# Attention and two gated feed-forward layers on one core: decay inputs in one transfer, decay matmuls apart from score matmuls, two operand differences in other buffers, and a new order

## The chip, the cores and the metric

The kernel runs on one core of one Trainium2 chip. The metric is device time in microseconds of one execution. Before the change it took 926.08 us, the median of three runs (925.92, 926.08 and 928.21 us).

## The reference

Inputs are q, k and v for 4 batches, 8 heads, 576 positions and head size 64, and s with one number per position. Each head computes

```python
scores = (q @ k.T) / sqrt(64)
cum    = cumsum(max(s, 0))                    # along the sequence
scores = where(causal, -1e9, scores + minimum(-(cum[i] - cum[j]), 0))
attn   = exp(scores - max) ; attn /= (sum + 1e-9)
out    = attn @ v
```

The result, 2304 tokens of 512 numbers, passes through two feed-forward layers, 512 to 2048 to 512: the first with h * clip(h + 3, 0, 6) / 6, the second with h * tanh(softplus(h)). All is float32. The word "decay" below means the term with cum.

## The kernel before

Nothing in the program is ordered where it is written. Each piece of work (a transfer, a matmul group, one vector operation) is recorded by `add` as a node with an engine, a cost, a priority, the nodes it depends on and the buffers it takes. `Plan.run`, at build time, walks a modelled clock and picks the ready node of the lowest priority number on each engine; where a node may run on ScalarE or VectorE it also picks the engine. The table `T` holds the priorities' offsets: `p0` to `p5` and `s0` to `s5` place the groups of attention heads, `xo1` and `lead1` place the operands and the weight sums of the first large matmul block, `w0` and `w1` the weights, and so on. The order that results is fixed; on the chip each engine runs its own list in order, and semaphores hold an instruction until what it needs is there. All loads and stores are issued from the SP queue, also in a fixed order. Where the model sees TensorE idle in its first 70 us, it puts in matmuls on the identity (L362), up to 24 in a place, whose result is not used.

Weights come as 64-bit floats. `rebuild` loads 512 KB of words into one of two buffers named `wraw` (L465) and makes float32 of it: one operation on ScalarE or VectorE (L434), then L444 and L461 on VectorE. Every operand of a large matmul is then split into a high part (a copy to fp32r, L367 on ScalarE or L371 on VectorE) and a low part (a subtraction on VectorE: L475 for weights, L926 for g, L1027 for x), and each product is made of three matmuls.

The sequence of stages:

- Setup: `s` is loaded four times, into four groups of 32 partitions (L386). `setup_cum` makes cum and its five rows (one per tile of 128 queries, shifted and times 8); `setup_parts` writes the first 384 elements into a tile `two` that holds a part per group, so that a matmul with a selecting column adds the decay to a score (L796).
- Small units, two heads at a time, over the first 256 queries. For batches 0 and 1 they are "fast": the scores (L794) and the decay (L796) go into the same PSUM bank as one node, then the row minimum with the causal mask on VectorE (L806), the exponential on ScalarE (L813), one over the sum (L821, L822), the normalisation (L831 on ScalarE, L833 on VectorE), transposes on TensorE (L839), their copies (L367), the product with v (L853), and a high and a low copy into `blk`.
- Units over the last 320 queries (scores L660, minimum L668, exponential L676, normalisation L696 or L698, transposes L707, v L730), spread over the first feed-forward layer of the first three blocks of tokens, whose matmuls are L911 (in) and L951 (out).
- `first_super`: a block of 2 x 2 tiles of tokens in the first layer, by seven products instead of eight. `operands` loads the four pieces x11, x12, x21, x22 and forms the differences t5 = x12 - x11, t6 = x22 - t5, t7 = x22 - x12, t4 = x21 - t6 (L1012) in buffers `xr`; `sums1` forms the sums of weights (L534, L519, halves L528). The matmuls are L1071, then L951 for the way out.
- The second layer in three such blocks (L1160, L1260).

## Time and profile before

| | |
|---|---|
| median of 3 runs | 926.08 us |
| the profiled execution | 926.9 us, of which the span 925.1 us |
| TensorE busy (matmul) | 907.6 us, 98% of the span |
| VectorE busy | 709.1 us, 77% |
| ScalarE busy | 597.2 us, 65% |
| GpSimd busy | 36.0 us, 4% |
| granted TensorE clock, mean | 0.998 of full speed |

The profiled execution's time stands 0.8 us above the median. A row of the timeline gives the start, the busy time, the engine, the source line, the tiles (out<-in), the shapes, how many instructions are merged, and in brackets the idle time before it and what ended it. PE is TensorE, PEld its weight loads, DVE is VectorE, ACT is ScalarE, POOL is GpSimd, SPq the queue that issues transfers.

### The profile page before, as it was taken

What the parts mean: (1) busy time and instruction counts of PE and PEld (TensorE: products, weight loads), DVE (VectorE), ACT (ScalarE), POOL (GpSimd) and SP (SyncE); (2) the same over time, 40 slices, a digit from 0 to 9 for tenths busy, and PEclk for the clock granted to TensorE, in tenths of its full rate; (3) what the DMA queues carried; (4) which work ended last, traced back from release to release, by engine and by line L of the source; (5) the groups of instructions that cost most, each with busy time, mean ns of one, the idle gap of its engine ahead of it and who ended that gap; (6) DMA issues with size and microseconds to landing.
All of it is one profiled execution on the core that took longest, in us unless ns stands there. A gap on an engine that the chain in (4) does not pass through costs nothing.

```text
span 925.1 us, 16487 instructions
## 1 busy us (share of the span) xinstructions
PE 907.6 (98%) x5278; PEld 790.5 (85%) x5278; DVE 709.1 (77%) x1756; ACT 597.2 (65%) x1352; POOL 36.0 (4%) x88
## 2 busy tenths in 40 slices
PE   6999999999999999999999999999999999999998
PEld 4677777777777788988888788999999999999998
DVE  6998778886696666379869985867967779677774
ACT  4987777776675577457666555766556665566553
POOL 0011111001000101000000000000000000000000
PEclk9999999999999999999999999999999999999999
DMA  8478888899787876530039998549874498744885
GB/s 276 152 233 282 293 295 255 297 372 355 255 315 290 290 237 211 199 115 23 1 94 362 391 379 298 165 145 317 256 245 128 136 305 258 245 130 129 255 255 183
DMA packets 112486, 217.90 MB, mean 236 GB/s; under 512 B 12848, under 2 KB 51792, under 8 KB 112400
## 3 DMA queue, kind: packets, MB, share of 16 engines
q1 hardware_dynamic: 112400, 216.85, 70.4%
q8 instruction: 42, 0.69, 0.3%
q14 instruction: 44, 0.36, 0.1%
HBM read 174.23 MB, written 42.57 MB: 234 GB/s over the span
## 4 chain that ended last, share of the span: by engine, by line
PE 91%; DMA 3%; ACT 3%; DVE 2%; issue 1%; SPq 0%; ACTq 0%; DVEq 0%
PE b L951 19%; PE b L1160 19%; PE b L1260 19%; PE b L911 12%; PE b L1071 8%; PE b L660 4%; PE b L730 4%; PE b L707 4%; DMA wraw<-in_w_out_dram 1%; ACT win L813 1%; PE b L853 1%; DMA wraw<-in_w_in_dram 1%; DMA ws<-xob 1%; PE b L794 1%; PE b L839 1%
## 5 line engine op out<-in xcount | busy, mean ns | idle before, releaser
L951 PE MATMUL b<-g,wo 128*128 128x512 f32 (+1 forms) x960 | 222.2, 374 | 0.1
L951 PEld LDWEIGHTS b<-g,wo 128*128 128x128 f32 x960 | 165.4, 189 | 33.1 <-issue 4.8
L911 PE MATMUL b<-blk,win 128*128 128x512 f32 (+1 forms) x576 | 134.0, 365 | 0.0
L1160 PE MATMUL b<-xob 128*128 128x384 f32 x654 | 122.7, 334 | 0.0
L1160 PEld LDWEIGHTS b<-xob 128*128 128x128 f32 x654 | 114.2, 188 | 0.3 <-ACT b L367 0.2
L911 PEld LDWEIGHTS b<-blk,win 128*128 128x128 f32 x576 | 94.4, 189 | 18.8 <-issue 5.8
L1160 PE MATMUL b<-xob,st 128*128 128x384 f32 x354 | 70.8, 334 | 0.0
L676 ACT ACTIVATE cb<-cb,nm 128x384 f32<-128x384 f32 (+2 forms) x80 | 54.5, 683 | 22.2 <-DVE nm L668 22.1
L1160 PEld LDWEIGHTS b<-xob,st 128*128 128x128 f32 x354 | 62.2, 188 | 0.0
L926 DVE TENSOR_TENSOR g<-e,g 128x512 fp32r<-128x512 f32 (+1 forms) x48 | 29.2, 608 | 42.5 <-ACT g L367 42.1
L482 DVE TENSOR_TENSOR xob<-xob 128x256 fp32r<-128x256 f32 x109 | 44.8, 420 | 20.2 <-ACT xob L367 18.3
L434 ACT ACTIVATE wtmp<-wraw 128x512 f32<-128x512 f32 x64 | 42.6, 670 | 20.3 <-DMA wraw<-in_w_in_dram 10.8
L1260 PE MATMUL b<-wo,xob 128*128 128x384 f32 x282 | 54.5, 334 | 0.0
L668 DVE CUSTOM_DVE_ANT_0 cb<-b,cb 128x384 f32<-128x384 f32 (+2 forms) x80 | 44.3, 587 | 11.9 <-PE b L660 9.5
L1260 PEld LDWEIGHTS b<-wo,xob 128*128 128x128 f32 x282 | 49.4, 188 | 0.0
L367 ACT ACTIVATE b<-b 128x384 f32<-128x384 f32 (+1 forms) x64 | 32.2, 504 | 23.5 <-PE b L1160 9.6
L1071 PE MATMUL b<-xob,wo 128*128 128x512 f32 x192 | 45.4, 390 | 1.5 <-ACT wo L367 1.4
L367 ACT ACTIVATE xob<-xob 128x256 fp32r<-128x256 f32 (+1 forms) x77 | 35.5, 464 | 13.8 <-DMA xob<-ws 12.2
L461 DVE SCALAR_TENSOR_TENSOR wtmp<-wraw,wtmp 128x512 uint32<-128x512 uint32 x64 | 43.9, 687 | 0.6
L1071 PEld LDWEIGHTS b<-xob,wo 128*128 128x128 f32 x192 | 35.8, 188 | 9.6 <-ACT wo L367 1.6
L660 PE MATMUL b<-qk 64*128 64x384 f32 (+2 forms) x288 | 43.9, 361 | 0.0
L367 ACT ACTIVATE g<-e 128x512 fp32r<-128x512 f32 (+2 forms) x40 | 22.0, 549 | 33.8 <-PE b L951 30.9
(199 smaller groups left out, 1762.3 us busy)
## 6 DMA issues: line engine op xcount, KB each, us to landing
xob<-ws SPq DMA_DIRECT2D x108, 256.0 KB, 3.4
wo<-wos SPq DMA_DIRECT2D x48, 512.0 KB, 5.2
wraw<-in_w_in_dram SPq DMA_DIRECT2D x32, 512.0 KB, 6.2
wraw<-in_w_out_dram SPq DMA_DIRECT2D x32, 512.0 KB, 6.0
st<-ws SPq DMA_DIRECT2D x60, 256.0 KB, 3.3
cb<-cula SPq DMA_DIRECT2D x16, 896.0 KB, 7.8
ws<-xob SPq DMA_DIRECT2D x56, 256.0 KB, 6.0
xob<-ws SPq DMA_DIRECT2D x109, 128.0 KB, 2.1
```

The source lines that it names most:

```text
L367: nc.scalar.activation(out=out_, in_=in_, func=AF.Copy)
L434: nc.scalar.activation(out=tmp.t, in_=hi, func=AF.Prelu, scale=2.0 ** -112, alpha=-(2.0 ** 32))
L461: nc.vector.scalar_tensor_tensor(out=out_, in0=lo, scalar=29, in1=tu, op0=ALU.logical_shift_right, op1=ALU.bitwise_or)
L482: return a, add("DVE", v1x(n), lambda: nc.vector.tensor_tensor(out=l(), in0=r(l()), in1=r(h()), op=ALU.subtract), [a], prio, (), [buf])
L660: nc.tensor.matmul(out=ps[g].t[:, 0:w], lhsT=t.t[s_, ka, qo:qo + P], rhs=t.t[s_, kb, nk0 + a:nk0 + e], start=k == 0, stop=k == 2)
L668: nc.vector.tensor_tensor_reduce(out=p.t[:, o:o + w], in0=pb.t[:, 0:w], in1=cb.t[:, o:o + w], scale=-0.125, scalar=(3.0e38 if a == 0 else ...
L676: nc.scalar.activation(out=p.t[:, o:o + w], in_=p.t[:, o:o + w], func=AF.Exp, scale=-1.0, bias=nm.t[:, k:k + 1], accum_out=l.t[:, k:k + 1],)
L911: nc.tensor.matmul(out=hps.t[:, 0:N], lhsT=w.t[:, a, P * c:P * (c + 1)], rhs=x.t[:, c, b, 0:N], start=(c == 0 and k == 0), stop=(c == NCC ...
L951: nc.tensor.matmul(out=y[j].t[:, co[j]:co[j] + N], lhsT=wt.t[:, a, P * j:P * (j + 1)], rhs=g.t[:, b, 0:N], start=(f == 0 and k == 0 and no ...
L1071: nc.tensor.matmul(out=bank.t[:, 0:N], lhsT=lhs(a, j), rhs=xo[p].t[:, j, c, :], start=start and j == 0 and k == 0, stop=j == 1 and k == 2, ...
L1160: nc.tensor.matmul(out=bank.t[:, 0:NS], lhsT=w.t[:, a, P * j:P * (j + 1)], rhs=xo[p].t[:, j, b, :], start=start and j == 0 and k == 0, sto ...
L1260: nc.tensor.matmul(out=banks[m].t[:, 0:NS], lhsT=w.t[:, a, P * m:P * (m + 1)], rhs=b.t[:, c, :], start=start and f == 0 and k == 0, stop=f ...
```

## The change

The host lays `s` out four times, one copy under the other, and one transfer of 128 partitions takes the place of four of 32; it is issued ahead of the first q and k instead of behind it. The factor 8 goes into the same operation as the maximum with zero. What was one node for the first half of cum and one for the second becomes several: the first half with the row of tile 1, the parts for `two` (in two pieces), the second half's maximum, its scan, and one node for each remaining row. The row of tile 0 becomes a copy.

For the fast small units the score matmuls and the decay matmuls are two nodes instead of one; the scores no longer wait for `two`, and the buffer of q and k comes free when they are done.

In the first large block t5 and t6 take the two `wraw` buffers instead of `xr`, and the group of matmuls for product 2 of the first step comes ahead of those for products 6, 5 and 7.

The planner's model of SP transfers in its first 16 us changes, and so do 23 entries of `T`, among them `xo1` (5.675 to -16.0), `lead1` (6.099 to 3.54), `s2` (23.451 to 14.468) and `p5` (94.699 to 103.271). Line numbers grow by 7 to 15 after the change.

```diff
...
-                        ring = max(now + 1.1, ring) + n.lat
-                        n.end = ring + 1.7
+                        ring = max(now + 1.1, ring) + n.lat * (1.35 if now < 16.0 else 1.0)
+                        n.end = ring + (1.0 if now < 16.0 else 1.7)
...
-        for k in range(4):
-            nc.sync.dma_start(out=rows()[0][NB * NH * k:NB * NH * (k + 1)], in_=s)
+        nc.sync.dma_start(out=rows()[0], in_=s)
...
-    def setup_cum(a, e, tiles):
-        s_sb, one, cum, crow = rows()
-        nc.vector.tensor_scalar(out=s_sb[:, a:e], in0=s_sb[:, a:e], scalar1=0.0, scalar2=None, op0=ALU.max)
+    def setup_pos(a, e):
+        s_sb = rows()[0]
+        nc.vector.tensor_scalar(out=s_sb[:, a:e], in0=s_sb[:, a:e], scalar1=0.0, scalar2=8.0, op0=ALU.max, op1=ALU.mult)
+
+    def setup_scan(a, e):
+        s_sb, one, cum, _ = rows()
         nc.vector.tensor_tensor_scan(
             out=cum[:, a:e], data0=one[:, a:e], data1=s_sb[:, a:e], initial=cum[:, a - 1:a] if a else 0.0, op0=ALU.mult, op1=ALU.add)
...
     def setup_parts():
-        crow, h = rows()[3][:, 0:384], two.t[:, 0:384]
-        nc.vector.tensor_copy(out=h, in_=crow)
-        nc.vector.scalar_tensor_tensor(out=h, in0=r(h), scalar=low_col, in1=crow, op0=ALU.mult, op1=ALU.add)
+        _, _, cum, crow = rows()
+        for a, e, x in ((0, P, cum[:, 0:P]), (P, 384, crow[:, P:384])):
+            h = two.t[:, a:e]
+            nc.vector.tensor_copy(out=h, in_=x)
+            nc.vector.scalar_tensor_tensor(out=h, in0=r(h), scalar=low_col, in1=x, op0=ALU.mult, op1=ALU.add)
...
-        n_s = A("PE", 1.0 if fast else 0.76, mm, [n_ld, n_m, *(n_id if fast else [])], prio, pss + [nm, l] + ([cb] if fast else []), [raw, two] if fast else [raw])
+        n_s = A("PE", 0.62 if fast else 0.76, lambda: score(True, False), [n_ld, n_m], prio, pss + ([] if fast else [nm, l]), [raw])
+        if fast:
+            n_s.mode = 1
+            n_s = A("PE", 0.38, lambda: score(False, True), [n_s, *n_id], prio, [nm, l, cb], [*pss, two])
...
-            t = Buf("xr", [P, 2, NS], F32)
+            t = Buf("wraw" if not si and o in (5, 6) else "xr", [P, 2, NS], F32)
...
+            if f == 0:
+                n = g1(2, wv, Y, False, [c1])
+                swish(Y, f, 0, n, t + 2 * d)
...
-            n = g1(2, wv, Y, False, [c1])
-            swish(Y, f, 0, n, t + 5 * d)
+            if f:
+                n = g1(2, wv, Y, False, [c1])
+                swish(Y, f, 0, n, t + 5 * d)
...
-        n_c2 = add("DVE", 2.6, lambda: setup_cum(256, S, (2, 3, 4)), [n_c1], PRO + T["cum"], (), [setup_a, setup_b])
...
+        n_c2 = add("DVE", 0.32, lambda: setup_pos(256, S), [n_p2], pc, (), [setup_a])
+        n_c2 = add("DVE", 0.88, lambda: setup_scan(256, S), [n_c2], pc, (), [setup_a])
...
+        n_c2 = [add("DVE", 0.45, lambda t=t: setup_row(t), [n_c2], pc, (), [setup_a, setup_b]) for t in (2, 3, 4)]
...
-        "qk1": qk1, "qk": qk, "v1": v1, "s": s.reshape(NB * NH, S),
+        "qk1": qk1, "qk": qk, "v1": v1, "s": np.tile(s.reshape(NB * NH, S), (4, 1)),
```

What the planner makes of it shows in three places. First ScalarE, from its first instruction on, before the change (L434 is a weight rebuild, L813 an exponential of the heads whose sums are l_197 or l_240, L831 a normalisation):

```order
L384 ACT_TABLE_LOAD
L434 ACTIVATE wtmp_235<-wraw_170 128x512
L434 ACTIVATE wtmp_258<-wraw_172 128x512
L813 ACTIVATE win_198,l_197<-win_198,nm_196 128x128
L813 ACTIVATE win_198,l_197<-win_198,nm_196 128x256
```

And after it, ScalarE from its first instruction on (L824 is the exponential, L441 the rebuild, L842 the normalisation):

```order
L384 ACT_TABLE_LOAD
L824 ACTIVATE win_225,l_224<-win_225,nm_223 128x128
L824 ACTIVATE win_225,l_224<-win_225,nm_223 128x256
L824 ACTIVATE win_225,l_224<-win_225,nm_223 128x128
L824 ACTIVATE win_225,l_224<-win_225,nm_223 128x256
L441 ACTIVATE wtmp_279<-wraw_167 128x512
L824 ACTIVATE win_247,l_246<-win_247,nm_245 128x128
L824 ACTIVATE win_247,l_246<-win_247,nm_245 128x256
L842 ACTIVATE win_225<-win_225,l_224 128x256 x2
```

Two rebuilds stood ahead of all exponentials. Now four exponentials come first, one rebuild follows them, and the second rebuild stands after the first copies of transposes (L367). Up to the first of these copies the old list has two rebuilds, nine exponentials and two normalisations of 128 columns, the new one has one rebuild, nine exponentials and two normalisations of 256.

Second TensorE, behind the first row of identity matmuls, before (L794 scores and L796 decay of the first pair of heads, in banks b6 and b7, and of the second pair in b4):

```order
L794 MATMUL b6_194<-st_144 128x128
L794 MATMUL b7_195<-st_144 128x128
L796 MATMUL b6_194<-G1_159 128x128
L796 MATMUL b7_195<-G1_159 128x128
L794 MATMUL b6_194<-st_144 128x256
L794 MATMUL b7_195<-st_144 128x256
L796 MATMUL b6_194<-G1_159 128x256
L796 MATMUL b7_195<-G1_159 128x256
L794 MATMUL b4_237<-st_157 128x128
```

And after, in the same place (L801 scores, L804 decay):

```order
L801 MATMUL b6_176<-st_152 128x128
L801 MATMUL b7_177<-st_152 128x128
L801 MATMUL b6_176<-st_152 128x256
L801 MATMUL b7_177<-st_152 128x256
L801 MATMUL b4_211<-st_154 128x128
L801 MATMUL b5_212<-st_154 128x128
L801 MATMUL b4_211<-st_154 128x256
L801 MATMUL b5_212<-st_154 128x256
L804 MATMUL b6_176<-G1_156 128x128
```

The old order needs the decay (G1 is the tile `two`) after two score matmuls; the new one does the scores of two pairs first. 24 identity matmuls stood ahead of this place and 88 in the whole program; now there are 21 and 79.

Third VectorE at the entry of the first large block, before (L1012 the differences, L1027 low parts of x, L926 the low part of g in the last block before, L528 the low half of a weight sum):

```order
L1012 TENSOR_TENSOR blk_4840<-blk_3647 128x1024
L926 TENSOR_TENSOR g_4850<-e0_4795,g_4850 128x256
L1012 TENSOR_TENSOR blk_4840<-blk_3647,blk_4840 128x1024
L1012 TENSOR_TENSOR blk_3647<-blk_3647 128x1024
L926 TENSOR_TENSOR g_4874<-e0_4828,g_4874 128x256
L1012 TENSOR_TENSOR blk_3647<-blk_3647,blk_4840 128x1024
L1027 TENSOR_TENSOR xob_4634<-blk_4840,xob_4634 128x2x512
L528 TENSOR_TENSOR wo_4903<-wtmp_3746,wo_4903 128x256
```

And after (L1023 the differences, L1038 low parts of x, L934 and L937 the last steps of the block before):

```order
L1023 TENSOR_TENSOR wraw_4720<-blk_3615,wraw_4217 128x1024
L371 CAST xob_4725<-blk_3615 128x2x512
L1038 TENSOR_TENSOR xob_4725<-blk_3615,xob_4725 128x2x512
L937 TENSOR_TENSOR g_4741<-e0_4665,g_4741 128x256
L1023 TENSOR_TENSOR blk_3615<-blk_3615 128x1024
L934 SCALAR_TENSOR_TENSOR e0_4766<-e0_4766,b4_4684 128x256
L937 TENSOR_TENSOR g_4773<-e0_4695,g_4773 128x256
L1023 TENSOR_TENSOR blk_3615<-blk_3615,wraw_4720 128x1024
```

The first difference (t5, in wraw_4217) now stands 61 rows further ahead; before, all four stood here, in the buffer blk_4840 or behind its first use. All seven low parts of x now come ahead of the first low half of a weight sum; before, four of the seven came behind it. Between the last of these low parts and the last copy of attention's result VectorE has 3 differences, 7 low parts, 1 copy to fp32r and 8 operations of 256 columns. On TensorE the last product with v (L730, now L737) has come nearer to the block: 93 matmuls of 256 columns lie between it and the first L1082 (the old L1071).

## Rows read from the trace of the kernel before

**Rows 1.** Busy time by stretch: stretch, length, each engine's busy time (instructions), granted clock, DMA.

```profile
0.00:80.00 80.00, 67.82 (x480) 49.73 (x482) 66.97 (x243) 61.97 (x185) 7.67 (x20) 0.98 0.73 230
80.00:400.00 320.00, 319.79 (x2024) 251.60 (x2021) 227.43 (x588) 213.38 (x486) 28.35 (x68) 1.00 0.81 279
400.00:416.00 16.00, 14.46 (x81) 12.10 (x80) 15.06 (x25) 10.82 (x20) 0.00 (x0) 1.00 0.30 91
...
40.00:60.00 20.00, 18.96 (x124) 14.08 (x123) 17.89 (x51) 19.00 (x54) 1.32 (x2) 1.00 0.64 197
```

**Rows 2.** Groups of TensorE by line and form: count, busy us, mean ns, idle before.

```profile
L362 PE MATMUL b<-ident 128*128 128x256 bf16 x88 | 13.4, 304 | 4.6 <-ACT win L367 2.6 <-POOL ident masks.py:199 1.4 <-DVE e L923 0.6
```

**Rows 3.** Timeline of the opening: start, busy, engine, line, [idle before <-releaser].

```profile
1.18 1.80 SPq L386 DMA_DIRECT2D pt<-in_s_dram  x4
...
5.20 0.29 DVE L402 TENSOR_SCALAR pt<-pt 128x256 f32<-128x256 f32 x1 [3.13 <-DMA pt<-in_s_dram]
...
7.17 0.62 DVE L420 SCALAR_TENSOR_TENSOR G<-G,low_col,pt 128x384 fp32r<-128x384 f32 x1
...
8.98 1.24 DVE L406 TENSOR_SCALAR pt<-pt 128x384 f32<-128x384 f32 x3
...
10.14 0.28 DVE L806 CUSTOM_DVE_ANT_0 win<-b,cmask 128x128 f32<-128x128 f32 x1
```

**Rows 4.** Transfers issued from 0 to 1.5 us and from 2.9 to 3.5 us: KB each, us to landing.

```profile
st<-in_qk_dram SPq DMA_DIRECT2D x1, 256.0 KB, 2.8
...
st<-in_qk_dram SPq DMA_DIRECT2D x2, 256.0 KB, 3.7
```

**Rows 5.** Timeline of ScalarE from its first work on, with one row of VectorE.

```profile
11.09 0.68 ACT L434 ACTIVATE wtmp<-wraw 128x512 f32<-128x512 f32 x1 [9.08 <-DMA wraw<-in_w_in_dram]
...
12.35 0.68 ACT L434 ACTIVATE wtmp<-wraw 128x512 f32<-128x512 f32 x1 [0.57 <-DMA wraw<-in_w_in_dram]
...
12.94 0.38 ACT L813 ACTIVATE win<-win,nm 128x128 f32<-128x128 f32 x1
...
14.81 0.17 DVE L821 TENSOR_SCALAR l<-l 128x4 f32<-128x4 f32 x1 [2.03 <-ACT win L813]
...
17.41 0.83 ACT L367 ACTIVATE win<-b 128x384 f32<-128x384 f32 x2
```

**Rows 6.** Busy time by stretch: TensorE empty, then at a lower clock.

```profile
14.00:16.00 2.00, 0.00 (x0) 0.00 (x0) 1.15 (x7) 2.00 (x10) 0.00 (x0) 1.00 0.99 324
...
18.00:20.00 2.00, 1.70 (x9) 0.91 (x10) 2.00 (x7) 2.00 (x8) 0.00 (x0) 0.50 1.21 250
```

**Rows 7.** Timeline around 75 to 80 us, where the opening ends.

```profile
75.74 0.66 ACT L434 ACTIVATE wtmp<-wraw 128x512 f32<-128x512 f32 x1 [1.72 <-DMA wraw<-in_w_out_dram]
...
79.69 0.87 PE L853 MATMUL b<-qk 128*64 128x256 f32 x8 [1.43 <-DVE nm L806]
```

**Rows 8.** Timeline at the entry of the first large block.

```profile
373.12 4.33 PE L730 MATMUL b<-pt,v 128*64 128x320 f32 x40
...
398.56 1.22 DVE L1012 TENSOR_TENSOR blk<-blk 128x1024 f32<-128x1024 f32 x1 [0.32 <-PE b L911]
...
400.52 1.55 PE L1071 MATMUL b<-xob,win 128*128 128x512 f32 x6
...
406.56 4.81 PE L1071 MATMUL b<-xob,wo 128*128 128x512 f32 x18 [1.39 <-ACT wo L367]
...
408.14 3.49 DVE L1027 TENSOR_TENSOR xob<-blk,xob 128x1024 fp32r<-128x1024 f32 x3
```

**Rows 9.** The same place: busy time of the stretch ahead, a word load and its first use.

```profile
377.00:400.00 23.00, 23.00 (x198) 22.90 (x193) 9.85 (x19) 8.46 (x17) 0.00 (x0) 1.00 0.67 229
...
382.36 0.91 SPq L465 DMA_DIRECT2D wraw<-in_w_out_dram  x2
...
464.22 0.65 ACT L434 ACTIVATE wtmp<-wraw 128x512 f32<-128x512 f32 x1
```

More of the change, by code (lines that the diff above doesn't have):

```diff
@@ L398, in setup_one, with setup_row @@
         nc.vector.memset(eps_col, 1e-9 / P)
[L400 to L402 removed]
+    def setup_pos(a, e):
[3 more added lines that the diff above has]
+        s_sb, one, cum, _ = rows()
         nc.vector.tensor_tensor_scan(
             out=cum[:, a:e], data0=one[:, a:e], data1=s_sb[:, a:e], initial=cum[:, a - 1:a] if a else 0.0, op0=ALU.mult, op1=ALU.add)
[L405 to L409 removed]
+    def setup_row(t):
+        _, _, cum, crow = rows()
+        o = crow[:, COFF[t]:COFF[t] + CW[t]]
+        if t:
+            nc.vector.tensor_scalar(out=o, in0=cum[:, 0:CW[t]], scalar1=cum[:, P * t - 1:P * t], scalar2=None, op0=ALU.subtract)
+        else:
+            nc.vector.tensor_copy(out=o, in_=cum[:, 0:CW[0]])
     def setup_sel():
@@ L787, in small, with score @@
         pss = [Bank(banks) for _ in range(2)]
-        def mm():
+        def score(first, last):
             for i in range(2):
                 o, e = P * i, P * i + CW[i]
-                for g in range(2):
+                for g in range(2 if first else 0):
                     q = raw.t[D * g:D * (g + 1)]
-                    nc.tensor.matmul(out=pss[g].t[:, o:e], lhsT=q[:, P * i:P * (i + 1)], rhs=q[:, N:N + CW[i]], start=True, stop=not fast)
-                for g in range(2 if fast else 0):
+                    nc.tensor.matmul(out=pss[g].t[:, o:e], lhsT=q[:, P * i:P * (i + 1)], rhs=q[:, N:N + CW[i]],
+                                     start=not fast or i == 0, stop=not fast, skip_group_check=fast and i > 0)
+                for g in range(2 if last else 0):
                     nc.tensor.matmul(out=pss[g].t[:, o:e], lhsT=two.t[D * g:D * (g + 1), 384 + row + g:385 + row + g].to_broadcast([D, P]),
-                                     rhs=two.t[D * g:D * (g + 1), o:e], start=False, stop=True)
-        n_s = A("PE", 1.0 if fast else 0.76, mm, [n_ld, n_m, *(n_id if fast else [])], prio, pss + [nm, l] + ([cb] if fast else []), [raw, two] if fast else [raw])
+                                     rhs=two.t[D * g:D * (g + 1), o:e], start=False, stop=True, skip_group_check=i > 0)
+        n_s = A("PE", 0.62 if fast else 0.76, lambda: score(True, False), [n_ld, n_m], prio, pss + ([] if fast else [nm, l]), [raw])
+        if fast:
+            n_s.mode = 1
+            n_s = A("PE", 0.38, lambda: score(False, True), [n_s, *n_id], prio, [nm, l, cb], [*pss, two])
         n_s.mode = 1
```

27 lines of the change are left out of this document (12 added, 15 removed).

## The prediction

> **What bounds the kernel now.** I read the busy time by stretch first. TensorE is idle for 17.5 us of the span of 925.1. Of these 12.2 lie before 80 us, 0.2 between 80 and 400, 1.5 between 400 and 416 [rows 1], and the 3.6 that are left lie behind its last matmuls. The matmuls themselves are the same before and after, form by form, except those on the identity. So the time is the useful matmul work plus what TensorE does not spend on it, and that lies in two places.
>
> The first is the opening. In 0 to 80 us TensorE is busy 67.82 us, so 12.2 are idle, and 13.4 us of the busy time are the identity matmuls [rows 1, 2]: 25.6 us in all without useful work. In that stretch the reader is to see ScalarE and VectorE nearly full: 19.00 and 17.89 us of the 20 from 40 to 60 [rows 1]. They are the bound of the opening, as soon as both have work. They get it late: VectorE waits until 5.20 us for the last transfer of s and makes its first row minimum at 10.14 [rows 3]; ScalarE's first work is at 11.09 and its first exponential at 12.94 us, because two weight rebuilds stand ahead in its list, and each waits for its words [rows 5]. VectorE then waits 2.03 us more for these exponentials [rows 5].
>
> The second is the entry of the first large block: 1.5 us of the 16 from 400 to 416 us are lost [rows 1], 1.39 of them at 406.56 before the matmuls of product 6 [rows 8]. VectorE is busy 15.06 us of these 16, while it had 13 us free in the 23 us ahead [rows 1, 9]: its first operand difference begins at 398.56, released by the last L911 [rows 8], since its buffer is cut from the tile those matmuls read.
>
> **The change, part by part.** *The transfer of s.* Four issues took 1.80 us, the last landing released VectorE at 5.20 [rows 3]. The new transfer has 288 KB and goes out first, at about 0.75 us. The nearest row is 256 KB issued at that time, 2.8 us to landing; the same size behind a fuller queue took 3.7 [rows 4]. So it lands between 3.5 and 4.5 us; I take 3.7, as nothing is ahead of it. The first q and k move behind it; their matmuls follow 21 identity matmuls, which at 13.4 us for 88 [rows 2] and a start at 1.4 end near 5, so this costs nothing there. All transfers behind go out three issues, 1.35 us, earlier.
>
> *The decay's chain on VectorE.* From 5.20 to the end of L420 at 7.79 it took 2.59 us [rows 3]. The new chain has one row copy less (tile 0) and its two part operations in two pieces each; I take the same 2.5. So the decay is ready at 6.2 us instead of 7.8. Then the row minimum: before it came 2.35 us later, with 1.24 us of row copies in between [rows 3]; those copies now stand behind the minima, one copy of 128 columns comes in (about 0.2), so 1.3 to 1.4 us later: 7.6 us against 10.14. The matmuls are ready for it: the scores of two pairs are done by then, only the decay's four matmuls must follow 6.2.
>
> *ScalarE's order.* The first exponential comes at 7.9 to 8.0 us instead of 12.94. From there to its first copy of transposes at 17.41 it took 4.47 us, without a wait, for nine exponentials and two normalisations [rows 5]. The new list has the same nine, normalisations of twice the width (about 0.2 more) and one rebuild of 0.68 [rows 5], whose words landed at 11.09 and now 1.1 to 1.6 us earlier, near 9.8: a wait of 0 to 0.6 behind four exponentials (to about 9.7); I take 0.3. So the copy comes at 8.0 + 4.47 + 0.2 + 0.68 + 0.3 = 13.65 us, 3.8 earlier, with one rebuild (0.68) still to do: 3.1 us of lead. VectorE's lead is the 1.5 us of the transfer plus what goes of its 2.03 us wait: 1.5 to 3.5. What is late next is ScalarE itself: exponentials come faster out of VectorE than ScalarE takes them.
>
> *Does the lead last to 80 us?* Up to the first transposition of the larger units the two programs have the same useful matmuls of each line on TensorE, 13 against 13 final rebuild steps on VectorE and 44 exponentials each on ScalarE by their lists. With both engines nearly full [rows 1] a lead of 3 us moves the end of the opening by 3 us, unless something else sets the pace. Bounds: 0, if it does, and 5 us, if the waits of 1.72 and 1.43 us near 76 and 80 us [rows 7] go as well. I take 3.0, nearest to the rows of ScalarE.
>
> *Stores of the decay rows.* They wait now for the last row copy, some 6 us later on VectorE; queued behind them on SP are two loads of decay for later heads and two of weight words. The loads are for heads of batches 2 and 3, which follow all of 0 and 1, and the words' buffers are not free sooner; I take 0, at worst some tenths within the bounds above.
>
> *Entry of the large block.* t5 and t6 no longer wait for the last L911. In exchange the last product with v, which ended at 377.45 against a first L1071 at 400.52 [rows 8], now stands only 93 matmuls ahead: at 23.00 us for 198 [rows 9] 10.8 us. On VectorE behind it come 3 differences and 7 low parts at 1.16 to 1.22 us (3.49 for three [rows 8]), one copy of about 0.55 and 8 short operations at about 0.4, then two low halves of weight sums, 0.8: 16.3 to 17 us, and 0.5 for the copy ahead of it. TensorE needs 10.8 + two products of 1.4 + 21 small matmuls at 0.116 + 0.2 = 16.2 us until product 6. So it waits 0.6 to 1.3 us, 0.8 as I take it, in place of 1.39: a gain of 0.6, with bounds of +1.4 and -1. Behind the waiting product stand the last L951 and everything after, so this counts in full. The word loads that must wait for t5 and t6 went out at 382.36 and were used at 464.22 [rows 9]: 80 us of cover, some 50 of it left.
>
> *The rest of the order.* Between 80 and 400 us TensorE lost 0.2 us [rows 1]. A new order can only lose there; I take 0 and a bound of 2 us of loss.
>
> *Sum.* 3.0 + 0.6 = 3.6 us from the profiled execution's 926.9 is 923.3. That execution stands 0.8 above the median, so 922.5 against the 926.08.
>
> **A rule that speaks against it.** TensorE was empty from 14 to 16 us, and from 18 to 20 us its granted clock was 0.50, the 1.2 GHz level [rows 6]. The Trainium skill ("TensorE: Matmul & The Clock Gate", section "HAM oscillation — how this bites in real kernels") says that an engine that waits between short bursts is throttled again and begins the next burst cold; the trace agrees. For the sum the row is enough: a stretch of 2 us at the lower level takes 1 us of work from TensorE. The new opening has 9 identity matmuls less and so may have more such stretches between 10 and 24 us; two more would take 2 us, less what the idle time there absorbs: 0 to 2 us, and I take 0, since the row minima and exponentials, not TensorE, set the pace there.
>
> **Rivals.**
>
> *The lead is eaten before 80 us.* For it: the words come through two buffers, and at 75.74 us ScalarE waited 1.72 us for them, then TensorE 1.43 us at 79.69 [rows 7]; the second rebuild now stands later than before. Against it: their pace is set by VectorE's last rebuild step, which frees the buffer, and the steps stand at the same places in VectorE's list from the third on. Only the entry's 0.6 would be left: 926.9 - 0.6, less 0.8: 925.5. The clock as above leaves 3.6 - 2 = 1.6: 924.5.
>
> *More than the lead.* Both waits of rows 7 vanish too, and the entry runs without a stop: 3.5 + 1.4 + 1.4 = 6.3 us: 919.8. For it: a stall that a late chain made goes with the lateness. Against it: 1.43 us are VectorE's own load at that point.
>
> *Slower: the entry of the large block.* The 12 us of distance given up there (23 against 10.8) were cover. If attention's last heads reach VectorE late, each microsecond in which VectorE is further behind at the last product with v than I assume (nothing queued) is a microsecond of TensorE, beyond a slack of none. It decides from 6.4 us of backlog on; with 8 us the time is 922.5 + 8 = 930.5. Against it: VectorE had 13 of 23 us free ahead of the block [rows 9].
>
> **How the numbers follow.** A difference of 0.3%, 2.8 us, is about what a measurement of this kernel can tell from no change: below 923.3 is faster, above 928.9 slower. The forecast, 922.5 with a range of its own from 921 to 924, has 0.48, of which 0.40 lie below 923.3. The lead eaten has 0.21 and the clock 0.08, all within 0.3%. More than the lead has 0.15, all faster. The late entry, with losses elsewhere in the order, has 0.08, of which 0.07 slower. That makes faster 0.55, within 0.3% 0.38, slower 0.07. The range from 919.5 to 926.5 leaves out the slower case and the ends of the others.
>
> **What would show it.** Right: the first exponential near 8 us, the first copy of transposes near 13.7, the product with v that began at 79.69 us [rows 7] near 76.7, with about 22.5 us of TensorE's time not useful before it, and one wait under 1.3 us at product 6 of the large block. Wrong: a first exponential at 8 us and that product still near 80 (the lead eaten), a granted clock of 0.5 over much of 10 to 24 us, new idle time of TensorE between 80 and 400 us, or several microseconds before the first L1082 groups.

## The result, and the profile after

The changed kernel took 918.17 us, the median of four runs (916.75 to 920.70), against 927.14 us (925.92 to 928.82) of the kernel before beside it: ratio 0.9903, 95% interval 0.9884 to 0.9923. It is faster, as forecast, but by about 9 us where 3.6 were forecast, and it lies below the range of 919.5 to 926.5.

The profiled executions are 916.75 us (span 915.0) after and 926.9 (span 925.1) before. First, the busy time by stretch after, in the columns of [rows 1]:

```profile
0.00:80.00 80.00, 74.33 (x510) 54.56 (x511) 72.33 (x263) 67.47 (x200) 6.89 (x20) 0.98 0.74 252
80.00:400.00 320.00, 320.00 (x2030) 253.58 (x2029) 231.11 (x578) 218.56 (x490) 30.69 (x68) 1.00 0.81 278
400.00:416.00 16.00, 15.33 (x73) 12.37 (x73) 13.60 (x30) 11.53 (x26) 0.00 (x0) 1.00 0.10 34
```

and the identity matmuls after, which answer to [rows 2]:

```profile
L362 PE MATMUL b<-ident 128*128 128x256 bf16 x79 | 11.5, 297 | 4.5 <-ACT win L367 3.1 <-POOL ident masks.py:199 1.4
```

In the first 80 us TensorE's idle time falls from 12.18 to 5.67 us and the identity matmuls from 13.4 to 11.5: 8.4 us. The entry of the large block gives 0.87 (1.54 idle before, 0.67 now), the stretch from 80 to 400 us 0.2, the end 0.3, and the useful matmuls (all but those on the identity) 0.3. That is the 10.1 us between the two spans, so five sixths of the gain lie in the opening. The two profiled executions stand 0.2 and 1.4 us below the medians of their kernels, so the medians differ by 9.0.

The opening after, by the timeline, against [rows 3, 5, 7]:

```profile
0.74 0.38 SPq L385 DMA_DIRECT2D pt<-in_s_dram  x1
...
3.62 0.29 DVE L401 TENSOR_SCALAR pt<-pt 128x256 f32<-128x256 f32 x1 [1.56 <-DMA pt<-in_s_dram]
...
5.79 0.48 DVE L427 SCALAR_TENSOR_TENSOR G<-G,low_col,pt 128x256 fp32r<-128x256 f32 x1
...
7.36 0.27 DVE L817 CUSTOM_DVE_ANT_0 win<-b,cmask 128x128 f32<-128x128 f32 x1
...
7.67 0.40 ACT L824 ACTIVATE win<-win,nm 128x128 f32<-128x128 f32 x1 [5.65 <-DVE nm L817]
...
9.44 0.65 ACT L441 ACTIVATE wtmp<-wraw 128x512 f32<-128x512 f32 x1
...
12.93 0.85 ACT L367 ACTIVATE win<-b 128x384 f32<-128x384 f32 x2
...
71.83 0.66 ACT L441 ACTIVATE wtmp<-wraw 128x512 f32<-128x512 f32 x1 [0.79 <-DMA wraw<-in_w_out_dram]
...
72.43 0.87 PE L864 MATMUL b<-qk 128*64 128x256 f32 x8
```

Up to the first exponential all is as forecast: s on VectorE at 3.62 (3.7 forecast), decay ready at 6.27, the end of the row at 5.79 (6.2), first row minimum at 7.36 (7.6), first exponential at 7.67 (7.9 to 8.0). The first copy of transposes comes at 12.93 (13.65). But the product with v that stood at 79.69 us stands at 72.43, where 76.7 was forecast.

One execution of an opening differs from the next. The runs g1 and g2 below leave the opening of before as it is, and their first copies of transposes come at 17.72 and 16.65 us (17.41 in before). Differences of some tenths between single timelines are no more than that.

The entry of the block, against [rows 8]:

```profile
379.00 2.27 PE L737 MATMUL b<-pt,v 128*64 128x320 f32 x20
...
392.82 1.55 PE L1082 MATMUL b<-xob,win 128*128 128x512 f32 x6
...
398.33 1.55 PE L1082 MATMUL b<-xob,wo 128*128 128x512 f32 x6
...
406.72 1.67 PE L1082 MATMUL b<-xob,win 128*128 128x512 f32 x6 [0.67 <-ACT b L367]
```

### The profile page after: what moved, and what is told of

Read it like the earlier page. It is cut to its first block, busy times and chain, and to the rows that moved or that the text cites. A ratio compares the mean times of both kernels' runs of the same rounds, so it can differ in the third digit from the quotient of the medians.

```text
span 915.0 us, 16473 instructions
## 1 busy us (share of the span) xinstructions
PE 905.4 (99%) x5269; PEld 790.7 (86%) x5269; DVE 707.7 (77%) x1751; ACT 601.5 (66%) x1359; POOL 37.6 (4%) x88
## 4 chain that ended last, share of the span: by engine, by line
PE 97%; DVE 1%; ACT 1%; DMA 0%; issue 0%
PE b L962 22%; PE b L1175 19%; PE b L1275 19%; PE b L922 12%; PE b L1082 8%; PE b L667 4%; PE b L737 4%; PE b L714 4%; PE b L864 1%; PE b L850 1%; PE b L801 1%; PE b L362 1%; ACT win L824 0%; DMA pt<-in_s_dram 0%; ACT win L367 0%; DVE win L817 0%
## 5 line engine op out<-in xcount | busy, mean ns | idle before, releaser
L937 DVE TENSOR_TENSOR g<-e,g 128x512 fp32r<-128x512 f32 (+1 forms) x48 | 28.6, 598 | 26.8 <-ACT g L367 26.5
L441 ACT ACTIVATE wtmp<-wraw 128x512 f32<-128x512 f32 x64 | 42.5, 668 | 8.6 <-DMA wraw<-in_w_out_dram 3.4
L367 ACT ACTIVATE pt<-b 128x384 f32<-128x384 f32 (+2 forms) x92 | 42.8, 513 | 8.1 <-PE b L714 7.9
L367 ACT ACTIVATE b<-b 128x384 f32<-128x384 f32 (+1 forms) x64 | 32.2, 503 | 23.3 <-PE b L1175 10.2
L1082 PE MATMUL b<-xob,wo 128*128 128x512 f32 x192 | 45.5, 390 | 0.0
L367 ACT ACTIVATE g<-e 128x512 fp32r<-128x512 f32 (+2 forms) x44 | 24.8, 563 | 29.6 <-PE b L962 26.9
L367 ACT ACTIVATE xob<-xob 128x256 fp32r<-128x256 f32 (+1 forms) x77 | 35.3, 463 | 12.8 <-DMA xob<-ws 9.5
```

Source lines behind the costliest of these rows:

```text
L367: nc.scalar.activation(out=out_, in_=in_, func=AF.Copy)
L441: nc.scalar.activation(out=tmp.t, in_=hi, func=AF.Prelu, scale=2.0 ** -112, alpha=-(2.0 ** 32))
L1082: nc.tensor.matmul(out=bank.t[:, 0:N], lhsT=lhs(a, j), rhs=xo[p].t[:, j, c, :], start=start and j == 0 and k == 0, stop=j == 1 and k == 2, ...
```

## The experiments

Theory A: the early start sets the opening and passes on to the end. Theory B: the early start is worth itself, and the new order gives the rest. In the runs with a held order a node is moved in the finished order and the planner does not run again, so all else stands where it stood. `at(tag, k)` finds the k-th node of a kind: "b1" and "b3" are the first two instructions of a weight rebuild, "ex" the exponentials, "min" the row minima. Times are medians of 4 to 12 runs; ratios are against the kernel before, run beside them. "Over after" compares with the 918.17 us above. "The copy" is the first copy of transposes, "the product" the product with v that stood at 79.69 us.

**A late start in the new order (a1_late).**

```diff
     def setup_pos(a, e):
         s_sb = rows()[0]
+        if a == 0:
+            for _ in range(8):
+                nc.vector.memset(rows()[1], 1.0)
```

> The kernel after, every engine's order as it is, with eight memsets of 128x576 on VectorE ahead of its first instruction on s (about 0.54 us each by the memset row of the trace after, 4.3 us together): the decay, the first row minimum and the first exponential start about as late as before. Theory A (the early start sets the whole of the opening, and what it leads by grows on the way, 4.5 us at the first copy, 7.3 us at 72 us): 925 us, some 7 us over the 918.2 of after, and the product with v that stood at 72.43 us stands near 79. Theory B (the early start is worth only itself, the rest comes from the new order between 45 and 80 us): 922.5 us, that product near 76.7. Theory C (the order alone, with slack that takes up a late start): 918 to 919.5 us, that product within 1 us of 72.4.

923.24 us, ratio 0.9957 [0.9943, 0.9970]: 5.1 us over the 918.17. Its timeline:

```profile
11.74 0.40 ACT L827 ACTIVATE win<-win,nm 128x128 f32<-128x128 f32 x1 [9.73 <-DVE nm L820]
...
17.00 0.84 ACT L367 ACTIVATE win<-b 128x384 f32<-128x384 f32 x2
...
76.65 0.87 PE L867 MATMUL b<-qk 128*64 128x256 f32 x8
```

The first exponential comes 4.07 us later than after, the copy 4.07, the product 4.22: up to there the lead passes on one to one and does not grow. The time is 5.1 us longer, which the intervals don't tell from 4.2. With a first copy only 0.4 us ahead of the old one, the new order is still 3.5 us faster than the old. That is theory B, with the larger share on the start; 0.87 of the 3.5 is the entry of the large block, which runs as after here.

**Four transfers in the new order (a2_four_s).**

```diff
-        nc.sync.dma_start(out=rows()[0], in_=s)
+        for k in range(4):
+            nc.sync.dma_start(out=rows()[0][NB * NH * k:NB * NH * (k + 1)], in_=s[NB * NH * k:NB * NH * (k + 1)])
```

> The kernel after, every engine's order as it is, with s loaded again by four transfers of 32 partitions in place of one of 128. By the two traces the last of four lands near 5.2 us where the one lands near 3.6, so VectorE's first instruction on s starts some 1.6 us later. Theory A (the start sets all, and grows): 920 to 921.5 us. Theory B (the start passes on by itself): 919.5 us, 1.0 to 1.6 us over after. If the four transfers are not what was late: 918.2 us, and the instruction at 3.62 us stays there.

919.80 us, ratio 0.9922 [0.9909, 0.9936], 1.6 us over after. The way there was not the expected one:

```profile
4.15 0.29 DVE L402 TENSOR_SCALAR pt<-pt 128x256 f32<-128x256 f32 x1 [2.08 <-DMA pt<-in_s_dram]
...
8.61 0.29 DVE L818 CUSTOM_DVE_ANT_0 win<-b,cmask 128x128 f32<-128x128 f32 x1 [0.64 <-PE b L805]
```

s is only 0.53 us later, not 1.6. The row minimum is 1.25 us later since it now waits for TensorE: q and k are issued behind the three extra transfers, at 2.56 us in place of 1.18. The copy is 1.96 us later than after, the product 1.82. Part of the worth of the one transfer is the earlier issue of all that follows it.

**The rebuilds ahead of the exponentials, new order held (c1_rebuild_first).**

```diff
+        for k in range(2):
+            x = at("b1", k)
...
+            order.remove(x)
+            order.insert(order.index(at("ex", 0)) + 0, x)
...
```

> The kernel after, with one thing moved in ScalarE's order: the first two rebuilds of weight words (two instructions of 128x512) stand ahead of the first exponential, as before. They wait for raw words that landed near 9.1 us in the trace before. So the first exponential starts near 10.5 us or later, not 7.7. If that place on ScalarE is what held the old opening: 921 us or more (2.4 to 4 us over after), the product with v of 72.43 us near 75 to 76. If the late decay on VectorE is the cause: 918 to 919 us.

922.55 us, ratio 0.9950 [0.9938, 0.9963], 4.4 us over after. (The 9.1 us of the expectation is the length of ScalarE's idle time in before, 9.08; the words released it there at 11.09.)

```profile
9.17 0.68 ACT L450 ACTIVATE wtmp<-wraw 128x512 f32<-128x512 f32 x1 [7.15 <-DMA wraw<-in_w_in_dram]
10.41 0.67 ACT L450 ACTIVATE wtmp<-wraw 128x512 f32<-128x512 f32 x1 [0.57 <-DMA wraw<-in_w_in_dram]
10.98 0.39 ACT L836 ACTIVATE win<-win,nm 128x128 f32<-128x128 f32 x1
...
15.67 0.84 ACT L376 ACTIVATE win<-b 128x384 f32<-128x384 f32 x2
...
47.42 0.38 ACT L376 ACTIVATE blk<-b 128x256 fp32r<-128x256 f32 x1 [2.17 <-PE b L877]
...
77.72 0.87 PE L877 MATMUL b<-qk 128*64 128x256 f32 x8
```

The copy comes 2.74 us later, and ScalarE's place for the rebuilds is a large part of the start. But the product is 5.29 us later (75 to 76 us was expected, 77.72 came), so here the lead is not passed on one to one: 2.55 us were lost behind the copy. One place shows it. From 44 to 48 us the granted clock of this run was 0.59,

```profile
44.00:48.00 4.00, 4.00 (x22) 2.52 (x22) 2.15 (x11) 1.83 (x8) 0.00 (x0) 0.59 0.41 139
```

after TensorE had waited 1.93 us for ScalarE before 43.91, and ScalarE then waited 2.17 us for TensorE at 47.42. After has the same wait of 1.94 us, a clock of 1.00 behind it, and at this place

```profile
42.48 0.39 ACT L367 ACTIVATE blk<-b 128x256 fp32r<-128x256 f32 x1 [0.97 <-PE b L864]
```

So some 1.2 us of the loss go with the clock, not with the place of the rebuilds.

**Parts of the early start in the old order (c2_exp_first, a3_one_s, d1_both_old).** c2 moves the first two rebuilds behind the fourth and the eighth exponential, a3 loads s by one transfer (its four copies laid in one input), d1 does both; the order is the old one otherwise.

```diff
+        for k, j in ((1, 7), (0, 3)):                      # c2, d1
+            x = at("b1", k)
+            order.remove(x)
+            order.insert(order.index(at("ex", j)) + 1, x)
...
-        for k in range(4):                                 # a3, d1
-            nc.sync.dma_start(out=rows()[0][NB * NH * k:NB * NH * (k + 1)], in_=s)
+        nc.sync.dma_start(out=rows()[0], in_=s)
```

> The kernel before, with one thing moved in ScalarE's order: the first two rebuilds of weight words stand behind the fourth and the eighth exponential in place of ahead of the first. If ScalarE's place is what held the old opening: its first exponential goes from 12.94 to about 10.5 us (it then waits for the first row minimum at 10.14) and the time falls by 1.3 to 2.4 us, to 924.7 to 925.8. If the late decay or the old order holds it: 927 us, no change. A fall by over 3.5 us would say that the rebuilds alone were the whole of it.

> The kernel before with its own order, and s by one transfer of 128 partitions. VectorE's first instruction on s should go from 5.20 to about 3.7 us, the row minimum from 10.14 to about 8.6. ScalarE's two rebuilds still stand ahead of its first exponential at 12.94 us and wait for words. If ScalarE's list sets the opening: 926.5 to 927 us, no change. If the decay does: 925.3 us, 1.5 less.

> The kernel before with its own order, but s by one transfer of 128 partitions (its four copies are laid in one input) and the first two rebuilds behind the fourth and the eighth exponential: the early start without the new order behind it. The row minimum should come near 8.6 us, the first exponential near 9, the first copy of transposes near 14.5 (17.41 before). If the early start is worth as much in the old order as in the new (5.1 us lost when it was taken away there): 922 to 923 us. If the old order behind it uses only a part, as the 0.85 us for some 2 us of earlier exponentials said: 924.5 to 925.5 us, and the rest of the gain needs the new order.

c2: 925.92 us, ratio 0.9990 [0.9980, 0.9999], less than the 1.3 to 2.4 us expected. a3: 925.76, 0.9985 [0.9976, 0.9994]; here the first exponential moved too, to 11.16 us, against what was expected, because the words of the rebuild landed earlier (its first instruction at 9.28 in place of 11.09). d1: 925.11, 0.9974 [0.9965, 0.9983]. d1's timeline:

```profile
9.58 0.40 ACT L823 ACTIVATE win<-win,nm 128x128 f32<-128x128 f32 x1 [7.57 <-DVE nm L816]
...
15.27 0.84 ACT L375 ACTIVATE win<-b 128x384 f32<-128x384 f32 x2
...
77.61 0.65 PE L864 MATMUL b<-qk 128*64 128x256 f32 x4 [1.04 <-DVE nm L816]
```

The copy is 2.14 us earlier than before, the product 2.08, the time 2.0. One to one again, so the old order does use a lead (c2 and a3 alone scatter about it: copies 1.35 and 1.78 us earlier, products 1.98 and 1.05); these two edits only make less than half of the 4.5 us. The other 2.3 us at the first copy (15.27 against 12.93) lie in what d1 leaves out. Two parts can be read off: s still goes out behind the first q and k and reaches VectorE at 4.31 us (3.62 after), and both rebuilds, not one, still stand ahead of the copy (0.65 us). The rest, 1.0 us, is the decay in pieces, its row copies behind the minima and the scores apart; only the row copies were tried alone (f1).

**The row copies ahead of the minima, new order held (f1_rows_first).**

```diff
+        rest = [x for x in order if x[0].tag == "row"]
+        order = [x for x in order if x[0].tag != "row"]
+        at = next(k for k, x in enumerate(order) if x[0].tag == "min")
+        order = order[:at] + rest + order[at:]
         self.order = order
```

> The kernel after, one thing moved in VectorE's order: the three row copies of the decay (1.24 us for the same three in the trace before) stand ahead of the first row minimum again. If the first row minimum sets the opening one to one: it goes from 7.36 to 8.5 us, the first copy of transposes from 12.93 to 14.0, the product with v of 72.43 to 73.5, and the time to 919.2 to 919.5 us. If the copies are free wherever they stand: 918.2 us.

919.08 us, ratio 0.9917 [0.9900, 0.9933]: 0.9 over after, in the expected size, but the interval also holds after's ratio. In the profiled run, the longest of its six (921.42 us), the first exponential was 1.32 us later, the copy 1.31, but the product 3.23 (75.66 us, where 73.5 was expected). As in c1 the clock fell near 44 us here, and ScalarE waited for TensorE:

```profile
44.00:48.00 4.00, 4.00 (x25) 2.77 (x22) 1.99 (x7) 2.58 (x9) 0.00 (x0) 0.71 0.24 95
```

```profile
45.15 0.38 ACT L372 ACTIVATE blk<-b 128x256 fp32r<-128x256 f32 x1 [1.96 <-PE b L870]
```

**Other tables and steps, the order made again (b1_new_table, a4_old_table, b2_joined).** b1 is the old code with the new `T`, a4 the new code with the old `T`; b2 is the new code with

```diff
-        n_s = A("PE", 0.62 if fast else 0.76, lambda: score(True, False), [n_ld, n_m], prio, pss + ([] if fast else [nm, l]), [raw])
-        if fast:
-            n_s.mode = 1
-            n_s = A("PE", 0.38, lambda: score(False, True), [n_s, *n_id], prio, [nm, l, cb], [*pss, two])
+        n_s = A("PE", 1.0 if fast else 0.76, lambda: score(True, fast), [n_ld, n_m, *(n_id if fast else [])], prio, pss + [nm, l] + ([cb] if fast else []), [raw, two] if fast else [raw])
```

> The code before with the new table of due times alone: s by four transfers, scores and decay in one step, the two differences in their old buffers; the planner makes a new order of it. If the new order comes from the table: 920 to 923 us, and the rebuilds stand behind exponentials. If it needs the edits of the code: 925 to 929 us, since the table's due times were set for another set of steps. The one that this tells apart is which part carries the order, not how the gain splits.

> The code after with the table of due times of before; the planner makes another order of it, with the same first forty instructions or so on ScalarE and VectorE. In the two orders run so far the stretch from the first copy of transposes to the product with v of the first batch's last heads took 62.3 us (old order, with an early and a late start) and 59.5 us (new order, the same). If the code's edits carry both gains: 917.5 to 919 us. If the start is the code's and the shorter stretch the table's: first copy near 13, and 921 us or more.

> The kernel after with score and decay matmuls as one step again, so that no scores run ahead of the decay; the planner makes the order again. If the apartness gives the scores nothing but an earlier place on TensorE: 918 to 919 us. If it carries part of the 2.4 us by which the first copy comes earlier than with the transfer and the rebuilds alone: first copy between 13.5 and 15 us, 919 to 921 us. Over 922 us: the new order behind hangs on it.

b1: 931.85 us, 1.0048 [1.0034, 1.0061]. a4: 930.92, 1.0041 [1.0026, 1.0056]. b2: 927.84, 1.0011 [1.0000, 1.0022]. None keeps the gain: table and code hold only together, and these three do not split it. a4 shows how such an order loses: its opening is nearly as quick as after's (copy at 13.03, product at 74.10, idle time and identity matmuls 18.5 us where before had 25.6), and then one wait near 390 us takes those 7.1 us back, in a4's timeline:

```profile
393.70 2.72 PE L962 MATMUL b<-g,wo 128*128 128x256 f32 x11 [6.99 <-DVE g L937]
```

**t5 and t6 in their old tile (b3_xr).**

```diff
-            t = Buf("wraw" if not si and o in (5, 6) else "xr", [P, 2, NS], F32)
+            t = Buf("xr", [P, 2, NS], F32)
```

> The kernel after, but the two operand differences (t5, t6) lie again in the tile that the last matmuls of the first large block read; the planner makes the order again, and it is the same up to that block. The wait at the entry was 1.39 us before and is 0.67 after. If that edit is what shortened it: about 1.4 us at the entry again, 918.9 us. If the new order shortened it: 918.2 us. Over 920 us would say that the new order behind the block hangs on it.

922.62 us, ratio 0.9954 [0.9940, 0.9969]: 4.4 us over after, more than either number expected. TensorE's waits in its timeline from 395 us on:

```profile
397.16 1.65 PE L1082 MATMUL b<-xob,win 128*128 128x512 f32 x6 [0.31 <-ACT b L367]
...
404.05 1.41 PE L1082 MATMUL b<-xob,wo 128*128 128x512 f32 x5 [0.61 <-DVE xob L1038]
...
407.72 1.66 PE L1082 MATMUL b<-xob,win 128*128 128x512 f32 x6 [0.67 <-ACT b L367]
...
479.90 80.41 PE L962 MATMUL b<-g,wo 128*128 128x512 f32 x351 [1.38 <-DVE win L1098]
```

The entry costs 1.59 us in place of 0.67, and a new wait of 1.38 stands 70 us later: 2.3 us that the edit saves. Of the other 2.1 some 1 us is the opening of that profiled run (73.39 us busy in 0 to 80 against 74.33, in the same order), and 0.8 us are two more of the matmuls that open a bank (L1091, four where after has two); the rest was not found.

**More identity matmuls (e1_more_identity).** Five more ahead of the second group of transposes, new order held.

```diff
+            if n is second:
+                self.warm(n.new[0].t, 5)
             n.fn(e) if len(n.eng) > 1 else n.fn()
```

> The kernel after, every order as it is, with five identity matmuls more ahead of the second group of transposes (near 11.7 us), where TensorE waits 1.20 us at 13.45 and the granted clock falls to 0.60 and 0.55 in 14 to 18 us. By those two rows the fall takes 1.7 us of TensorE's work. If the fall goes and its price is on the path: 916.5 to 917.2 us. If TensorE's speed at that place sets nothing, or the fall only comes elsewhere: 918 to 918.5 us.

917.94 us, ratio 0.9903 [0.9888, 0.9918]: no change. The granted clock did change. After, by stretch:

```profile
14.00:16.00 2.00, 2.00 (x14) 1.13 (x12) 1.61 (x7) 2.00 (x8) 0.00 (x0) 0.60 1.19 369
16.00:18.00 2.00, 2.00 (x12) 1.98 (x11) 2.00 (x8) 1.69 (x5) 0.00 (x0) 0.55 0.96 351
```

and in e1:

```profile
14.00:16.00 2.00, 2.00 (x20) 1.42 (x18) 1.82 (x8) 2.00 (x8) 0.00 (x0) 1.00 1.14 390
16.00:18.00 2.00, 1.68 (x17) 1.16 (x14) 2.00 (x9) 2.00 (x7) 0.00 (x0) 1.00 0.96 343
```

So the fall to near the 1.2 GHz level costs nothing at that place; the profiled execution of after, which has it, was at 916.75 us the shortest of all. It does not follow for other places: c1 and f1 show a fall near 44 us that others waited for.

**What in the old order is slower (g1_min_first, g2_rebuild_earlier, g3_all_old).** From the first copy to the product with v the old order takes 62.28 us (before) and 62.34 (d1), the new one 59.50 (after) and 59.65 (a1_late), with VectorE busy 55.1 to 55.7 us in all four. But the new order takes 62.05 and 61.42 us in c1 and f1, whose mean granted clock over the stretch was 0.93 and 0.94 (0.97 in before, d1 and after, 1.00 in a1_late), so the stretch is not a mark of the order alone. The VectorE waits that differ most are those for rebuilds, 2.9 us before and 0.8 after, by the views of waits (total, count, longest) of the two:

```profile
DVE wtmp L444 <- ACT wtmp L434: 2.9, 4, 1.4
```

```profile
DVE wtmp L451 <- ACT wtmp L441: 0.8, 2, 0.4
```

g1 puts the 14th rebuild behind the row minima of that product, g2 puts the first instruction of three rebuilds earlier on ScalarE, g3 does both and d1's two moves.

```diff
+        x = at("b3", 13)                                   # g1, g3: x and what hangs on it go behind y
+        y = at("min", 47)
...
+        order[p:q + 1] = [z for z in order[p:q + 1] if z not in move] + move
...
+        for k, j in ((6, 3), (7, 4), (12, 2)):             # g2, g3: j places earlier on ScalarE
+            x = at("b1", k)
+            acts = [y for y in order if y[1] == "ACT"]
+            ahead(x, acts[acts.index(x) - j])
```

> The kernel before with its own order, except that the two VectorE instructions of the 14th weight rebuild (the first waits 1.38 us for ScalarE at 76.43) and the copy on ScalarE that follows from them stand behind the four row minima of 79.00, as in the new order. If that place makes the longer stretch: the product with v goes from 79.69 to 77 or 77.5 us and the time falls by 1.4 to 2.5 us, to 924.3 to 925.4. If the rebuild that now comes later stops something else, or the product was not on the path: 926.8 us, no change.

> The kernel before with its own order, except that on ScalarE the first instruction of three weight rebuilds stands two to four places earlier (those of 48.65, 50.64 and 72.61 us, for which VectorE waited 0.80, 0.38 and 0.36). If these waits are part of the longer stretch: they go, the product with v of 79.69 comes 1.0 to 1.5 us earlier, and the time falls to 925.3 to 925.8. If ScalarE's other work, now later by as much, takes their place: 926.8 us, no change.

> The old order with all four moves: s by one transfer and the first two rebuilds behind exponentials (2.0 us together when tried), the 14th rebuild behind the row minima, and the three rebuilds earlier on ScalarE. If they add up: the stretch from the first copy to the product near 60 us, and 922 to 923 us. If one bound takes over from the other: 924 to 925 us, and the shorter stretch belongs to the new order as a whole.

g1: 927.46 us, 1.0007 [0.9995, 1.0019]. g2: 927.33, 1.0000 [0.9992, 1.0009]. g3: 925.41, 0.9983 [0.9973, 0.9993], as d1. In g1 the wait of 1.38 us went and came back elsewhere; in g2 the waits for rebuilds fell from 2.9 to 1.4 us, and VectorE waited 0.87 and 0.65 us for exponentials instead. In g1's timeline

```profile
77.77 0.83 DVE L970 TENSOR_TENSOR g<-e,g 128x512 fp32r<-128x512 f32 x1 [1.19 <-ACT g L404]
...
79.39 0.87 PE L897 MATMUL b<-qk 128*64 128x256 f32 x8 [0.33 <-DVE nm L848]
```

VectorE now stops for a gate copy, and the product is 0.3 us earlier, not 2. The order's own share does not sit in the VectorE waits that were moved.

**Scores back at their decay, new order held (h1_score_at_decay).** I then counted TensorE's useful matmul time from the start: its busy time by stretch less that of the identity matmuls in the same stretch (time at a lower clock counts in full). The last column counts the useful matmuls begun by 20 us.

| useful us up to | 20 us | 60 us | 120 us | matmuls by 20 us |
|---|---|---|---|---|
| before | 4.7 | 35.9 | 94.2 | 46 |
| d1_both_old | 7.2 | 38.0 | 96.7 | 62 |
| a1_late | 8.8 | 39.9 | 99.1 | 68 |
| after | 11.3 | 43.2 | 102.8 | 92 |

The late new order is ahead of the old one by 20 us already, by 4.1 us or 22 matmuls; the matmuls are the fairer count, since the granted clock of a1_late was 0.50 from 10 to 16 us. Eight of the 22 are scores, which TensorE does while it waits for the decay. And TensorE is full from 50 to 80 us in the new order but for 0.4 us. Before and a1_late in the stretch from 50 to 60 us:

```profile
50.00:60.00 10.00, 9.40 (x55) 7.20 (x55) 9.12 (x20) 9.12 (x23) 1.32 (x2) 1.00 0.79 244
```

```profile
50.00:60.00 10.00, 10.00 (x61) 7.30 (x59) 9.54 (x20) 8.20 (x18) 1.26 (x2) 1.00 0.73 258
```

(1.3 us of before's 9.40 are identity matmuls, none of a1's 10.00.) h1 takes the scores' place away:

```diff
+            order.remove(s)                                # s: a score step, x: its decay step
+            order.insert(order.index(x), s)
```

> The kernel after, one thing moved in TensorE's order: in the opening each score step (8 matmuls of a pair of heads, L801) stands directly ahead of its decay step (L804), so that no scores run ahead while TensorE waits for the decay or for transposes. The first row minimum needs only the first pair and stays near 7.4 us. If the scores that ran ahead are the order's head start: less useful matmul work at 20 us than the 11.3 of after, TensorE full later than 50 us, and 919.5 to 921.5 us. If they only fill time that was free anyway: 918.2 us.

920.35 us, ratio 0.9921 [0.9904, 0.9939], 2.2 over after, with a first copy at 13.06 (12.93 after), 9.8 us useful at 20 us (77 matmuls) and 100.2 at 120, and the product at 75.80 us. This interval and after's overlap; of the nine runs of after and e1 seven lie under 918.5 us, of h1's six one. So scores that don't run ahead seem to cost 1 to 3 us. Whether their place does it is not shown, since the granted clock differs too. From 12 to 20 us, after and then h1:

```profile
12.00:20.00 8.00, 6.80 (x49) 4.75 (x48) 7.33 (x28) 7.66 (x27) 0.00 (x0) 0.79 0.96 332
```

```profile
12.00:20.00 8.00, 7.29 (x45) 5.13 (x45) 6.34 (x27) 6.09 (x22) 0.00 (x0) 0.60 0.56 191
```

Runs of one kernel differ in their mean granted clock, and the time goes with it. The runs of before that stand beside these experiments took 928.2 us in the median at a mean clock of 0.994 (29 runs), 926.7 at 0.996 (53) and 925.7 at 0.998 (11). The one run of h1 at 1.000 took 918.30 us, no more than the two of after at that clock (917.94 and 918.40); its other five, at 0.996 and 0.998, took 919.65 to 921.26. One run settles little, but it leaves room for the scores' place to cost nothing by itself. The order's own share stays at equal clock: at 0.996 a1_late took 922.6 us in the median of four runs, 4.1 less than before.

No version tried is faster than the changed kernel by more than the spread.

## Why the prediction was wrong

*The opening's sum, the step that failed.* The prediction took 3.0 us for the whole opening: both programs have the same matmuls there, so "a lead of 3 us moves the end of the opening by 3 us", and the order behind the start stood in the sum at nothing. Idle time and identity matmuls fell by 8.4 us, and the product that marks the end of the opening came 7.26 us earlier, outside the bound of 5. Two terms make the difference: the lead was too small, and the order has a gain of its own.

*The lead, mechanism right, size too small.* A lead passes on about one to one to the product where nothing else changes (a1, a2, d1), though not where the clock falls again behind it (c1, f1). The first copy came 4.48 us earlier, and I took 3.0. Of the missing 1.5, 0.33 is the first exponential (7.67 for 8.0), 0.39 the stretch from there to the copy (5.26 us in place of the 5.65 I summed: the rebuild did not wait), and 0.68 is the second rebuild, which I took off the lead; what it costs at its new place was not measured by itself.

*The order, put at nothing.* With the start as late as before the new order is 3.5 us faster (a1_late), 0.9 of it at the entry. "A new order can only lose there; I take 0 and a bound of 2 us of loss" was said of 80 to 400 us, and there nothing was lost (0.2 us gained). But no term was there for the order inside the opening, which is worth some 2.6 us. I had looked at ScalarE and VectorE as the bound of the opening, and counted TensorE's idle time as their consequence. TensorE is full from 50 us on, so useful matmuls that it does in an earlier gap can come off the end, and the new order has more of them done by 20 us. My text saw the scores that run ahead only as "done by then". That they are the cause is not shown: h1 fits it, but its clock was lower too. What makes up the 2.6 is open; it is not TensorE's wait of [rows 7] (g1).

*The sum.* 2.0 for transfer and rebuilds (d1), 2.3 at the first copy for what d1 leaves out, and 3.5 for the order with the entry make 7.8 of about 9 us (a1_late's copy is still 0.4 us early, so that much is in both of the last two terms); what is left is within the spread of these medians and was not told apart.

*The entry.* Right in size: a gain of 0.87 us for the 0.6 taken. The wait of 0.67 does not stand at product 6 (398.33, no wait) but four groups of matmuls later (406.72, product 4), for a copy by ScalarE. That the two differences matter for more than the entry (b3) I did not see.

*The rivals.* "More than the lead" came nearest with 919.8 and had 0.15, too little. Its mechanism was the two waits of [rows 7]; TensorE's 1.43 us are gone and ScalarE's 1.72 are 0.79, yet with 1.1 of the 1.43 taken away in the old order (g1) the time is the same, so it was near by its number alone. The lead was not eaten, the clock of the profiled run fell in 14 to 18 us about as long as before (18 to 22 us) and cost nothing there (e1), and the large block did not come late.

## What to carry to other kernels

Where one engine is full from some point to the end, count an opening by the useful work that engine has done by then, not only by how much earlier its feeders start: work that needs no late input and moves into an early gap may come off the end. Count the work in matmuls done, since busy time grows at a lower clock, and compare runs at the same mean clock before you call a difference of 2 us the edit's. A new order is an unknown with two sides, and waits that a timeline shows in an order whose other engines are nearly full do not add up: taken away one by one they came back elsewhere. A table of due times belongs to one set of steps; moving it or a step alone took 9.7 to 13.7 us more than the pair.

## What the runs showed of the hardware

Three issues fewer at the head of the queue (1.35 us of issue time) brought the first rebuild's words earlier: at 9.28 us in a3_one_s, against 11.09, 11.46 and 10.07 in three runs with the old issues (before, g1, g2). Those three spread by 1.4 us, so the gain is 0.8 to 2.2 us.

```profile
9.28 0.66 ACT L433 ACTIVATE wtmp<-wraw 128x512 f32<-128x512 f32 x1 [7.26 <-DMA wraw<-in_w_in_dram]
```

```profile
10.07 0.66 ACT L461 ACTIVATE wtmp<-wraw 128x512 f32<-128x512 f32 x1 [8.06 <-DMA wraw<-in_w_in_dram]
```

Four transfers of s in the new program released VectorE at 4.15 us, one at 3.52 to 3.71 in eight runs, so 0.53 later than after and not 1.6: what came late were the transfers behind them. And a TensorE that waited early was granted the lower level of its clock again: 0.50 from 14 to 20 us in c1_rebuild_first, after 0.18 us of work in the 2 us before. What such a fall cost differed. In 14 to 18 us of after it cost nothing (e1); near 44 us ScalarE waited 2.17 and 1.96 us for TensorE in c1 and f1, where after has 0.97.
